# A second recorded order for a five-engine kernel of a long convolution and a SwiGLU block

## The chip, the cores and the metric

The kernel runs on one core of one Trainium2 chip. The metric is device microseconds (us) of one execution, the median of several; beside it stands one execution taken with the hardware profiler. Engines are PE (TensorE matmul), PEld (its weight loads), DVE (VectorE), ACT (ScalarE), POOL (GpSimd) and SP (SyncE, which here only issues DMAs).

## What is computed

```python
# S = 2048 tokens, D = 640, F = 1728, everything bf16
x  = A_q
h  = x + A(layernorm(x), k, v, shift_k, ssm_k, ssm_D)
h2 = h + (silu(layernorm(h) @ w_gate) * (layernorm(h) @ w_up)) @ w_down

def A(q, k, v, shift_k, ssm_k, ssm_D):
    k_shift = sum(k shifted down by i rows * shift_k[:, i] for i in 0..3)
    kv = k_shift * v
    y  = causal convolution of kv with ssm_k along S (length-2S FFT per channel)
    return q * (y + kv * ssm_D)
```

## The kernel before, in words

The 2048 tokens are four blocks j of 512; the 640 channels are two halves c of 320. A block's convolution is done with a 1024-point transform that is written as two small dense matmul stages, so it costs matmuls, PSUM evictions, elementwise products of spectra and SBUF-to-SBUF shuffles. All code is one function; every step is registered as an op with a name, and the names are used below:

- `kvm`, `kva`, `kvv` + jc (kv_block): the shift and the product kv, nine DVE operations of 128x1280 for each half.
- `s1X`, `s1K` + jc + b (fwd): first transform stage on PE, evicted by `e1..`; then `sh..G` DMAs that shuffle partitions; `s2X`, `s2K` + jc + G: the second stage, evicted by `e2..`. For block 0 the stages K01, X00 and X01 are done in one dense stage from the 1 MB table `full`, with no shuffle.
- `sw..` DMAs swap even and odd partitions; `m`, `a`, `q`, `x` operations on DVE multiply and add spectra (prods).
- `i2` + jc + G: first inverse stage on PE, evicted by `e3..` and shuffled by `rs..` DMAs; `i1` + jc + bp: second inverse stage. `q..`, `o..`, `h..`, `bn..`, `ag..` finish the first residual and the statistics of the second layer norm.
- `hn..` normalize; `tr..` (PE, block 0) or `hx..` (DMA, blocks 1 to 3) transpose; `gu` + j + i + bank: gate and up matmuls of feed-forward pair i, evicted by `si..`, `ue..`, multiplied in `gm..`; `dn` + j + b: down projection; `fa..` adds the residual, `st..` stores.

PSUM holds four two-bank tiles, two in pool pF and two in pool pC. SBUF pools have one to five slots, so many ops also wait for the last reader of the slot they take: KIN and VIN (loaded k and v) have one slot each, HT (input of `i1`) and the two TB tiles one each.

What sets the order is a table. `replay` (line 107) unpacks, from the string `_ORDER` (line 1133), the engine and a planned start for every op. Each engine's program is its ops sorted by planned start; there is no other scheduling, and every engine runs its list strictly in that order, waiting on semaphores. DMA issues stand in the same lists of SP, ACT or POOL, so a DMA that has to wait holds everything behind it on that queue. The planned starts do three more things:

```python
            o.lead = max(0, int(gap / (0.083 if o.start > cold else 0.166)))
...
            if held and max(held) > o.start - 1.0:
                continue
            k = bisect.bisect_left(work, (o.start - 0.2, 0)) - 1
            if k >= 0 and (not held or work[k][0] > max(held)):
                o.deps.setdefault(self.ops[work[k][1]], 2)
```

First, `lead` is a number of filler matmuls (128x192, line 521, results unused) that PE runs just ahead of an op, until the first `gu`, wherever the plan has PE idle. They are meant to keep its clock up, and they are part of PE's list: an op behind them starts after them even when its data is there. Second, a DMA that the plan issues late is given an artificial wait for an ACT or DVE op that ends about then. Third, the slot that a pool hands to a tile follows the planned order, so it decides which earlier reader is waited for.

Of the kernel before, what the change touches and what calls it, by code (L numbers as in the profile page):

```python
# [342 lines left out]
def bass_sequential_preLN__ssm_conv_h3__swiglu_ffn__prompt_kernel(  # L343
# [787 lines left out]

_INFO = None
_ORDER = (
    "c-pO#2UwHW8po6G3y_da_TGyuNJ0o?k_{w4AS93=OGHJ%0cxw#QneQMDr&1(rPhTLs#c#`N3FA3ZLO`>)oUw`)}mEvwT|Ly_1fOv-p6yE=e*~6&;K3g_ni-b"
    "!C)W&c`%_6C<uc>9#0q)27<kZFyNU1{=S3!F74I+5%%B!26@&2z#dpA<Z<BB`5@0l!k%+LpNj+mXz$sRetIRahpj&97=(e4#{=3c`=3nj`oQ!y`t0&B>0dMW"
    "qu1W?=ldtueCB4)c!9@PdBE)HGA|_glcY~4@1^%x^=S7(NIm)hz4dwp50`&L3HJ1hcm(C?*YTHvC(q!CeIX@*|0)3fhA8l&h(1CJ{+~pjZT(ODPku`16Wu@I"
    "2mEKEhuDDU3j=@hfu5lSJf;Qw?fO@oB+U7cYG?#f1&Kg7KqGJosslQpccCF*2@ruC@AX~)5MU257F2++7#wH={XlixQfMXG1ZxChp~s-R0WE42LLGMru{drU"
    "+!y;%EEzow`EL9~WB@Y*y&2tx=>n|ao8V>83TuH~hE0hX4DJTyF(YFtVy?tg!ZyUXVf$cdv4+^Su`}R{;tJs7<0$Y?;BLhCar@zm;F0(n@neyDka$!F5<umk"
    "W+8SUMj-AWir_!Rlj9c0Ns#ZM+~`&`9J3sA49&p|#2m%MVOy{jxHWhrkx$r!X~%8FH6#otU`gK+>@g!^yJEv}`{UT~2Dl1w9}L49W9nmLVo$}j#W$mL@tfj1"
    "5p&VSn1fg{?miB{<>SWSS0j|jX|aiMhfxtU7Rg3$LVbqagG(Yb5e^di6FwxoP8?2DCafjhBIS}Vl6R1sNU?-6GLABV(nAqZBa{lt2udTRjl!m;P*+h;QDrng"  # L1140
    "H9{RgJ50S!-A3!79i>U=_4Fgylaz4@?bI-9Cl^Y(#+}4D!vVQG-b~pp*-m+uVlI6c;}CrXqn!pa%IN8g>x|bK3)thBw;2xBQg#bV$a#~qhwm3G=U(D;3Z*=^"
    "=q)K;iV<%R(`3n#m9k0>lr0hN7p8M(iRfazs7+*$7-f9%4OwR*oZpYPLUuyX#XBlcB~~Y5mBUp9>JH5@bxBfl@=c9TOHxCU6`C~~P-~N?C=M$Js?5nFW9f)|"
    "@Fmn_Oag8^q7?fh>R0+bMizmEK8yYVvx=@~PhqhWj<d7aL)b&O?;y^@@$swT&BzwyWn>9T9bbdrh*x1>!7jsJ!{5Z%v8DtM@na%_7?1fBV?@tImt$sPI#J)E"
    "f><(kHr9-9CHz7-Pa=|$_$dA=j*EYfyahjs{5D}VrGly>en~w?Q_=y3lJ+*uz=V+V$P35^$dH7-33rHcQW-@?rqTtBjf@U@gt?xHW)-tGvk$Tq>>jp&2j>xa"
    "6#i9yg#aVe3uo{#qOF2a!f~SOqBkV#Bt+~)EER{vSK+_J%M-RGB$J%f8Ps~pN0gP6TNF6;Aax==p8h`bCuSTmmFOT|A(99#!fV70L@%938OhvD|B=aJRWs)@"
    "*Rig#&N6bDZ?KGP3Fin$%pJ+y&TZyh6&Qs_g>!^1kwV<gUnI~7Dg{%yr?^?X2|S9BBe*O4hPP65Q5+ImBugdTl8E%AL@u2#-5}eWs7{=kXppaz(-m7462ZO1"
    "eR6_gj^bOzJY|376a`YbT{%;^QAt(JR9RKsstz?y)uC!tgKDYzin=`MLeh?;G0A;WuIYwr?`lt{H0rkM_ot-jp@x>!z53S-)bv>G1YIcoUj|ajx%6GeRVIpg"
    "jfH02Xnxz;Cu4~oo!VrCo2I8Wn+{kS(}>0{+gH{WW43*<W4yWBTxuI+S!fAac^Q1iap%h}(DS`F=sxAX>z$Z+Dsy|rD|U)=gzM+5CXdCtB$J<|%T^|^X-Mj)"
    "v<&X6{Bb&38b5V}USxPRjcZnz@D@aRj8$$uX>BC#A*PZRkl3^aS_OSD!^UXff5QKqSHKT(7jto(Ce8`L0)bFcDe-VV<kYfT*^}5O*oQgyICF$u;^R`Lv_*Vg"
    "JX*X;%#uu#G)mV<7fWiyMA=souC!B%l$FcQ%LYno61x-2<@e>eiWKDug-}_W#8&QA9+fXu+Z9|DF)=SuC=bdzm7r>VuYZfetnjP0s^Zl>YD?0aNvD&<$zzhg"  # L1150
    "NS0~d(uB0^)FT?YcCt1@dp2dVc9@>28>U-lOSVNV2<t7|TN!x{se@$Cw=c2wSU1~Wa&)_HI_#`l%z3OUtN{BA+sa$c*NI|eBV=b)iE5+j8`Y1AGv(@}2DMXn"
    "F=dPTqWXMNYVtNknR1a@nAD*8C0VcO(DfvXG<Z#gW}xnb?wmGFzfUXHx9PX)z?7Dh9({AFHI;4{V%Te7rCmx}mM*k$(`(YZtgY!U87HQ#Gj*j`n{K6FHU3~^"
    "ni@>snP!+qn@5?38+M!Ln$<?B#b;}?HCfJ@(bn14i`GdQCo)9#{EXI&3mH2ywz?7acJCQ`tLKzstz(s=$Ki6m?EKQX#@XQ<<NU^v?7ZjHxWw-5E|DwZy5OpF"
    "&2drOH{5b}foF<4>Snv!-JR~Q-F}bNTj8nm9`TIJ>&{!1OU|1bIFolLaM<VZ^~*V$v&<jJ-I;sZAM&FLYVu2S^ub6N$X=Qq4crUN^G(g~Q!uYkURV+aL(~vh"
    "w7E!@)sm$v+7~8g1I43@w+Fil#)U=}ejl_Hg5kNv%OVS-!jhAH78kK2>gf9Du3AJ1txsZUdnvSRR!Li*d8O2{x-vTln_REFFZVg4Mx`%3a6flV?zFtc0cPRs"
    "pr*It<ihoZ!jOzl6*LP<h3^aB5r3ierCimy(`KbDH5^K-HJmo=O1BtomNZk3?N{UL*7LT}sh3k{TMk(qwtAa3qpy9f^Nu6dp?4g#@iIzX(_IssVpo&nYgf?I"
    "<EiwTGjDj0WDd^SnT7L3eO<n~>@C>}AKaVj6?p5tHJR5k_j-T!uFp1Qg?#bZt9{-6IDejhnSVh}L#{b6J7CTY<SocM6h0Kr4=yjH6!kB<UX)*K4SyDD4%Ua}"
    "hA)O^6j_Uorb_jnr3KS}G5O7P_Dc6FmUo<&oflkV-7NP9ZjXJqV|X^)BlPdfIp@`6R(U!+6EinvVzMk*A7s_|R`@pN8vQl?U49^^(|6sMne$zaFDETGKgXT7"
    "FmFZRZtjgdL;ivMmkT~FKozblxLt5KxHoV!a4zs#{_%W5!L@u|!SVb-1)(51xH>qy@MK|6Fex-KBnpoR?+SN^(!vwMjADJUthm1T<KmmeibybWyLfe^tT-uh"
    "ECP?3qE*qckx7xIk=DqrNK(`pZHc}c<(AxzLQ7aBq!MGvqLPl1^CkZ-DeW`9ic-btKczpcA8Nquis=<M`&SJZQ~BM1P38QG_P*A>Z58q=PjzSYih;x$ZU2^<"  # L1160
    "%yL-SkpZTG2g*MjSY7#fWnI6M{R;X<t525=E9<T*E&r)3wR~v5rW(>9M(x5{NL}k7(cra%)wL69adp#&kcZA6dSz&H?fg34khUQ=hx`VQutdZ"
)


# [26 lines left out]
```

## Time and profile before

| what | value |
|---|---|
| median of 5 runs | 305.59 us (303.33 to 310.04) |
| the profiled execution's own time | 304.88 us |
| its span, first to last instruction | 303.0 us |
| PE busy | 279.7 us (92%), 1696 matmuls, 74 of them fillers |
| DVE busy | 235.7 us (78%), 413 instructions |
| ACT busy | 184.4 us (61%) |
| POOL busy | 22.6 us (7%) |
| DMA | 52.08 MB in 55292 packets |

PE's busy time counts the modelled, overlapping length of matmuls. The distance from one matmul's start to the next is the better measure, and the trace gives it for all 1696. At full clock it is 136 ns for 320 columns, 216 ns for 512 and 83 ns for a filler; in parts of the first 75 us it is twice that (267 ns and 160 ns).

### The profile page before, as it was taken

How to read it: one execution, taken by the hardware profiler on the slowest of the kernel's cores; microseconds unless marked ns; L12 is line 12 of the kernel's file. 1: busy time of each engine (PE TensorE's matmuls, PEld its weight loads, DVE VectorE, ACT ScalarE, POOL GpSimd, SP SyncE). 2: the span in 40 equal slices, each digit the busy share in tenths (PEclk: the TensorE clock that was granted, in tenths of full speed). 3: DMA queues.
4: the chain of work that ended last, by engine and by line, in shares of the span. 5: the costliest groups of instructions: out<-in, count | busy, mean ns of one | idle time of the engine just before them, and what ended most of it. 6: DMA issues, size and time to landing. Idle time of an engine off the chain costs nothing.

```text
span 303.0 us, 4816 instructions
## 1 busy us (share of the span) xinstructions
PE 279.7 (92%) x1696; PEld 162.0 (53%) x1696; DVE 235.7 (78%) x413; ACT 184.4 (61%) x273; POOL 22.6 (7%) x29
## 2 busy tenths in 40 slices
PE   7799977387999999998999999999999999999993
PEld 4655544145555555664454567754554675444671
DVE  2798989769979998999989999969799963033322
ACT  3556676548799878763899878857887521511000
POOL 0000022012040000120000200100002010000000
PEclk9999999879999999999999999999999999999998
DMA  7967699958889957998724344558221132000011
GB/s 226 312 186 254 225 271 253 298 209 240 300 262 343 278 208 219 285 178 274 240 108 130 110 153 135 148 190 267 110 108 45 44 78 75 0 0 2 0 66 43
DMA packets 55292, 52.08 MB, mean 172 GB/s; under 512 B 19923, under 2 KB 49140, under 8 KB 55269
## 3 DMA queue, kind: packets, MB, share of 16 engines
q1 hardware_dynamic: 53444, 46.47, 49.0%
q0 software_dynamic: 960, 3.41, 4.6%
q10 hardware_dynamic: 864, 1.90, 1.9%
q8 instruction: 13, 0.21, 0.3%
q14 instruction: 11, 0.08, 0.1%
HBM read 19.00 MB, written 2.62 MB: 71 GB/s over the span
## 4 chain that ended last, share of the span: by engine, by line
PE 64%; DVE 15%; DMA 10%; ACT 4%; issue 4%; SPq 1%; ACTq 0%
PE ps L498 62%; DVE sb L507 12%; DMA sb<-sb 6%; ACT sb L481 4%; DMA sb<-in_A_k_dram 2%; DVE stt L761 2%; DMA tab<-cst_tab 1%; SPq L489 1%; PE ps L521 1%; PE ps L630 1%; DVE stt L765 1%; ACT sb L484 0%; DVE sb L783 0%; DVE stt L776 0%; ACTq L489 0%
## 5 line engine op out<-in xcount | busy, mean ns | idle before, releaser
L498 PE MATMUL ps<-sb 128*128 128x320 bf16 (+3 forms) x1128 | 209.9, 337 | 3.8 <-DMA sb<-in_A_k_dram 1.2
L507 DVE TENSOR_TENSOR sb<-sb 128x1280 bf16<-128x1280 bf16 (+2 forms) x238 | 174.0, 768 | 13.7 <-ACT sb L1056 3.4
L498 PEld LDWEIGHTS ps<-sb 128*128 128x128 bf16 (+3 forms) x1128 | 108.8, 98 | 86.4 <-issue 4.3
L481 ACT ACTIVATE sb<-ps 128x640 bf16<-128x640 f32 (+1 forms) x134 | 90.5, 714 | 37.9 <-PE ps L498 35.6
L498 PE MATMUL ps<-sb,tab 128*128 128x320 bf16 x450 | 79.4, 305 | 10.6 <-ACT sb L481 3.7
L498 PEld LDWEIGHTS ps<-sb,tab 128*128 128x128 f16 x450 | 41.7, 99 | 42.3 <-issue 7.2
L507 DVE TENSOR_TENSOR sb<-ps,sb 128x640 bf16<-128x640 f32 (+3 forms) x34 | 29.1, 860 | 41.1 <-PE ps L498 39.0
L1040 ACT ACTIVATE sb<-ps 128x1024 bf16<-128x1024 f32 (+2 forms) x32 | 29.3, 917 | 27.3 <-PE ps L498 27.2
L484 ACT ACTIVATE sb<-ps 128x640 bf16<-128x640 f32 x29 | 19.5, 703 | 10.8 <-PE ps L498 10.7
L1056 ACT ACTIVATE sb<-ps 128x1024 bf16<-128x1024 f32 x18 | 18.4, 1022 | 9.1 <-PE ps L498 7.1
L761 DVE BATCH_NORM_STATS2 stt<-sb 128x6 f32<-128x320 bf16 x48 | 22.4, 483 | 0.1
L784 ACT ACTIVATE sb<-sb,stt 128x320 bf16<-128x320 bf16 (+1 forms) x26 | 19.1, 754 | 4.2 <-DVE stt L776 3.4
L774 POOL TENSOR_TENSOR stt<-stt 128x2 f32<-128x2 f32 (+1 forms) x10 | 10.7, 1071 | 67.4 <-DVE stt L772 52.7
L521 PE MATMUL ps<-sb 128*128 128x192 bf16 x74 | 10.5, 299 | 2.9 <-ACT sb L481 1.4
L521 PEld LDWEIGHTS ps<-sb 128*128 128x128 bf16 x74 | 7.8, 118 | 5.4 <-ACT sb L481 2.4
L482 DVE CAST sb<-ps 128x640 bf16<-128x640 f32 x6 | 4.8, 821 | 4.3 <-PE ps L498 4.2
L783 DVE TENSOR_SCALAR sb<-sb,stt 128x320 bf16<-128x320 bf16 (+1 forms) x22 | 7.9, 380 | 0.1
L810 POOL TENSOR_TENSOR stt<-stt 128x4 f32<-128x4 f32 x2 | 3.1, 1530 | 59.7 <-DVE stt L808 59.7
L803 ACT ACTIVATE sb<-sb,stt 128x640 bf16<-128x640 bf16 x8 | 6.6, 827 | 0.0
L796 ACT ACTIVATE sb<-sb 128x640 bf16<-128x640 bf16 x8 | 5.9, 734 | 0.0
L765 DVE BATCH_NORM_AGGREGATE stt<-stt 128x2 f32<-128x12 f32 x24 | 4.3, 196 | 0.0
L489 POOL DMA_DIRECT2D tab<-cst_tab x2 | 1.3, 634 | 35.8 <-ACT sb L481 25.2
(29 smaller groups left out, 30.8 us busy)
## 6 DMA issues: line engine op xcount, KB each, us to landing
sb<-sb SPq DMA_DIRECT2D x144, 160.0 KB, 2.5
sb<-in_A_k_dram SPq DMA_DIRECT2D x5, 560.0 KB, 5.0
out_dram<-sb SPq DMA_DIRECT2D x16, 160.0 KB, 2.1
sb<-in_A_q_dram SPq DMA_DIRECT2D x3, 640.0 KB, 5.0
sb<-sb SPq DMA_DIRECT2D x24, 80.0 KB, 3.0
sb<-in_B_w_up_dram SPq DMA_DIRECT2D x3, 480.0 KB, 5.2
sb<-in_B_w_down_dram SPq DMA_DIRECT2D x3, 480.0 KB, 5.3
sb<-in_A_v_dram SPq DMA_DIRECT2D x4, 320.0 KB, 4.3
```

The costliest lines, as they stand in the source:

```text
L481: fns = {"act": lambda a: a.activation(out=dst(), in_=src(), func=ACTF.Copy), "dve": lambda v: v.tensor_copy(out=dst(), in_=src())}
L484: fns = {"act": lambda a: a.activation(out=dst(), in_=src(), func=ACTF.Copy, scale=scale), "dve": lambda v: v.tensor_scalar(out=dst(), in0 ...
L498: return lambda t: t.matmul(o(), l(), r(), start=st, stop=sp)
L507: return lambda v: v.tensor_tensor(out=o(), in0=a(), in1=b_(), op=op)
L521: P.fill = lambda t, pt: t.matmul(B32(pt, 1, 192), V(GUT, 13 * 512 + 256, 128), V(GUT, 13 * 512, 192), start=True, stop=True)
L761: vec(dve1(CW, False), lambda v: v.bn_stats(st6(l, j, b, c), V(xt, b * D + c * CW, CW)), [(xt, (b, c))], [(ST, ("s", j % 2, b, c))], prio, ...
L765: vec(0.16, lambda v: v.bn_aggr(ag(l, j, b), st6b(l, j, b)), [(ST, ("s", j % 2, b, c)) for c in range(2)], [(ST, ("a", j, b))], prio, name ...
L774: P.op({"pool": 0.95}, lambda g: g.tensor_tensor(out=y, in0=va, in1=stt[:, 288:288 + hi - lo], op=ALU.pow), c1 + [(ST, "half")], c3, prio, ...
L783: "dve": lambda v: v.tensor_scalar(out=dst(), in0=src(), scalar1=tmv(l, j, 5)[:, b:b + 1], scalar2=rs(l, j, b), op0=ALU.add, op1=ALU.mult),
L784: "act": lambda a: a.activation(out=dst(), in_=src(), func=ACTF.Identity, scale=rs(l, j, b), bias=tmv(l, j, 3)[:, b:b + 1])},
L1040: P.op({"act": act_c(n)}, lambda a: a.activation(out=dst(), in_=src(), func=ACTF.Silu), rd, wr, -1000, name=f"si{j}{i}")
L1056: P.op({"act": act_c(1024)}, lambda a: a.activation(out=V(ut, 0, 1024), in_=B32x2(u, 512), func=ACTF.Copy), [(u, 0), (u, 1)], [(ut, 0)], - ...
```

## The change

Only the string `_ORDER` differs. The functions, the set of ops, their shapes and their data dependences are the same. The diff, cut:

```diff
 _ORDER = (
-    "c-pO#2UwHW8po6G3y_da_TGyuNJ0o?k_{w4AS93=OGHJ%0cxw#QneQMDr&1(rPhTLs#c#`N3FA3ZLO`>)oUw`)}mEvwT|Ly_1fOv-p6yE=e*~6&;K3g_ni-b"
...
+    "c-pO#2UwHm7J$hhWG93qBxI1ifJ_oX0!awjB#=NzNJ2tnh%!__Y_Iavs@3bNlWOa#qu5^cs;ISfkGikp7OjKY)=|;cs<^M#;sr-9wt8!yr{Dkl=bY#J&N<&X"
...
 )
```

Unpacked, the new table does this:

- **Engines.** 18 ops go from DVE to ACT (the evictions tap0, tap1, e300G2, e330G2, e331G0, e2X31G1, e2X31G2, e2K31G3 and ten norms `q`). 13 go from ACT to DVE (the evictions e2X10G0, e1X20b0, e1K30b2, e330G0, e330G3, e331G1, e2K31G1, e2K31G2, e2X31G3, three norms `q`, and hn23).
- **DMA queues.** tab1, tab3 and wdl go from POOL to SP; tab2, shK00G0, shK00G2 and rs00G1 from ACT to SP; shK00G1, rs00G0, rs01G0 and rs01G1 from SP to ACT; x1, kin21, x2, kin31 and vin31 from SP to POOL.
- **First part, SP.** ident and drow stand ahead of kin0 and kraw00; vin10 and kin10 are issued right behind `full`, ahead of the first shuffles; the transposing load kx10, which followed x0, is now behind shK00G2 and shK00G0. vin10 has an artificial wait for he01, and x0 for the first kvm00.
- **Fillers.** 76 for 74, elsewhere: 23 (for 14) before the tap matmuls, none (for 5) before hl01, 2 before ktr00, 21 (for 4) before ktr01, none (for 3 + 3 + 9) up to s1X10, 2 (for 8) before i1001, 4 before i201G3 (14 before s1X11b2 gone), 5 (for 10) before i1010, 14 (for none) before s2K10G1, none (for 4) before s1K11, 3 + 2 around tr00.
- **Local swaps.** PE's order changes by neighbours in most places: i200G1 comes one dense stage earlier, i201G1 before i1000, s1X11b0, s1X11b2 and s2X10G3 before s2K10G0. Up to the first `gu` PE has the ops that it had there before, and i210G0 besides; the order of the feed-forward pairs is nearly the same.

More of the change, by code (lines that the diff above doesn't have):

```diff
@@ L1133 @@
 _ORDER = (
-    "c-pO#2UwHW8po6G3y_da_TGyuNJ0o?k_{w4AS93=OGHJ%0cxw#QneQMDr&1(rPhTLs#c#`N3FA3ZLO`>)oUw`)}mEvwT|Ly_1fOv-p6yE=e*~6&;K3g_ni-b"
-    "!C)W&c`%_6C<uc>9#0q)27<kZFyNU1{=S3!F74I+5%%B!26@&2z#dpA<Z<BB`5@0l!k%+LpNj+mXz$sRetIRahpj&97=(e4#{=3c`=3nj`oQ!y`t0&B>0dMW"
-    "qu1W?=ldtueCB4)c!9@PdBE)HGA|_glcY~4@1^%x^=S7(NIm)hz4dwp50`&L3HJ1hcm(C?*YTHvC(q!CeIX@*|0)3fhA8l&h(1CJ{+~pjZT(ODPku`16Wu@I"
-    "2mEKEhuDDU3j=@hfu5lSJf;Qw?fO@oB+U7cYG?#f1&Kg7KqGJosslQpccCF*2@ruC@AX~)5MU257F2++7#wH={XlixQfMXG1ZxChp~s-R0WE42LLGMru{drU"
@@ L1138 @@
[L1138 to L1161, printed above, removed]
+    "c-pO#2UwHm7J$hhWG93qBxI1ifJ_oX0!awjB#=NzNJ2tnh%!__Y_Iavs@3bNlWOa#qu5^cs;ISfkGikp7OjKY)=|;cs<^M#;sr-9wt8!yr{Dkl=bY#J&N<&X"
@@ new lines @@
+    "?|*(E7z_phV*pPd5E$^>1V3NE7Z&JOE9QT$fPP_p2Yvd54RD_mFs3i8_ppDynBPSLejf?=Z6pZTn+@>1p1xv1Pih7Asopo{*#h*sy_V{geF_Nvjd+q240;s<"
+    "aDQ6Av!4|9yiIU_CNJy)pSAM5rPoUic)jF(IG@1-^rQF8>#6mZkODmc4+8Wq;1lsGO2C&k)qf(MLg_ypuXK1>d#}mv)mH-l^p*XI_Fn$i5bYa0(ElR}{NvH+"
+    "%?y0ma6D}Z`0MNe|HSM8UzX_EX9d2v|KzWKJzBs&l&|8nf^t8m1`v$tdnN$KfldRVplv`4Xe;OvxH9GwKxND<&~DIT&?Qg=%#1w}>w`EzTc9I=WvIvC(*PoH"
+    "Iq(?Rgld4nVHcovP%G>*d_NL|*2A(;W6)jb_t0C=^_Y_&4tNy!ORz9@bnK~EF@yqc0xyNc$6bl_#8p9#LqL$(kZ<A^$9))gA2td0IqW8MBuoy!2Hy)C3WvZA"
@@ new lines @@
+    "h|`FjNE|APnuI)oWTNb_HSku%9t0l&K;DXz!Li7VC<MA4O~KS)8qwdPMVLd_HtZQJC%zmvH(@+J5etYP8}CS1jo(3-OV|r}6GDw^j5{31g3f_nflZ1%AA14P"
+    "85e~<g04XrkW}P6)L8gE^g=W?J{V8OEx^u=|33ahxE4_pr-9u^veA{OOQ<8LAeM-uCVZ1nM(9j<4}TFK#^)2iBB~P?kxr0$Nc9PA2~$XX@;LHV@_R{5<Wb~*"
+    "l0PMPl5>;%NqCBl(n{Hxlu0S3xF}7ORH}hGow}QfrhSLqPF|gGIH@$5$0if+u#P2j7!TQM&fwGx;ik0vX%DFxbSEu_UO=5in?OBC8%xL2Madu0vB{|nA9H51"
+    "owbx5=Em@v*&VF6dH2|R_@h!VDQ5*^g^yCQMGdKV)&@ok{|ryWrU@d#D}1luy6}V43Sm;(`LuU9Bn~re0~gLs<t<6ulU6AGKz2dis*ETA=^K>+)ge`rd~!NY"
@@ new lines @@
+    "iBe5fjTMI__oP3{bm@{<0hj`vj%vkV;=OP)<|J+)^)3yGZ^i`BwS-1`4gD7?E4iK7!{9LYGUvg}@P+Vc2qtnQ@)oil)dO$Cb>q4)`PfT1X#x-XF197%YXXz7"
+    "kWhn}hmoU~qOYM(VJ@R8&=puNb_w=!{35~;!qLQ@#BK4Dao@+6;2fk2I5&w&$V)nqbQ&L~Y@#fqc2mjJO6of54~bc%JW>m(FoA}T63|2=c^`>EKTjD+kENZY"
+    "S0~>~wli88JCfmy4u*|$j(wi(=a9J5xFFtq!EDaYoMpUgJSRU_G(x;lgu?E??8Y|5ABumB+nu1o+ll*0@#K5tl}WS7KPHuuKPHc$s410ndh%?%hY%)yLA;2^"
+    "5opBmL@_NVaVh;AeF&YAJc)ju{yyUXLq;1zo0?2y4rlFT`PeY_FYF3V9Z$?(&o}ei`1OKITs7|?_W@VWp2!Ze4|5*y^gNefBX6Hzkq|4qBMgb!L=7o3MVCa1"
@@ new lines @@
+    "lsbN@@ZGf2X^X`K$y5nIdXYa;z?1w<B9ji3mdmb6Mbe=3qV%j3AnTM>$g%PRa<k%sEL}cRK1set-lABaeoc|6Y)QYUenb68H7KJd^GXIyTadXWbGx=so2AiZ"
+    "Ey$jsLa4DiQPvdo44q#;D#v4(W+dd&jB|3An_D#k4PC!WZ`T?PUl~=|>vXG33v(yyJr;?TW;|_xnI0Lh=9r8JO_wc0ZFalQamdMbtaKc47Px@!@n(Ug%Sy0M"
+    "br$5Ioei#AE_Z$)VOr94GLp8E)x+$_SdevFb3r>_)0#awN32iD`6T<O@wPG1^b<itoI$)w>>{tHx@jwDb+m4dmdoe9!Ck<*&iaChVtv5{@Ky@03LY?pEG@H^"
+    "$zZNvj$y53ZQ+gJH1ktZcM7@%)xuwdHsNmJ9T7JrPjr*NCgq%{R-{gOCxwyPp4yQDO%sR@i7CA-H%Ko@+N5`-c-d5$PI5}|xg<*tNjok^NHmhSWXEL{vRN{P"
@@ new lines @@
+    "Y>g~MK12GxT&$R)V5AR8-;|C~)++ZX*{XU~cV<AfN)@Bd&KRLyt_ozH%t%u!O?9TrIirm*bBkGKnP$0QCR<E7+l*C~jh0$#tMzemdvcJ`&Ok8BnMatpT%oWc"
+    "b#*F4zFD3vzb|)+=ZbeLV$z`*mW(b1RB2Q+DmtZb8AP#0fmL-V^Hu9IM=Rr0^OT2_H!`lPPh_NIsxsfn5NmFzFqzq!4oz75KzlpWo7J7=$X=EW*3}r#WasKq"
+    "jSafFdbX~`fY3_}%k@9%r|7%%O2ZPvHp5Q_t-+zq%-L_)u8ZdIOruTXj4N|+xkGag=H{E1nZ*{8xx&28yu&&nugkp9dCu~{F0|gV46|;wqHSi|N48NmtL-h@"
+    "TI<i&i?%xZzwK@IuWiR{Rd%#pVP9llXK!{89A_N)4vXU-jwO!$4rkt%dC@$Kb5>rbcZj#E2vxMUc$Ig8Z=5^Py`)fC81XQR<`f}3vpi>g#lG={;*z&RRr$IC"
@@ new lines @@
+    "OYzZSx%-4~mA^XhbBQKY61);P9CDU+<UerXN|%QU3+9*33UBnYN{$D<Dp^`03gm>Yg=@=hmo-O8<)ceSM0z4!WxnzO(dzOW<-;mIYWgACFyP^UQRN-wJDJ#Y"
+    "rC2X*w64(Hafgb*-hdZYyw?W}%<?Pz%>j5&65J77&Dq4Q<Hhis`C!4Mj9qG-`f)GkIa#-}Vzf)LT68ycpBO(gY|?*d8k74VSEX&!J~T>lXP9=Hy3J_wTedn2"
+    "%Cg?lY<g_EZ{yp&woh#UYm@yK$A9wN&IPW^PGkQ3d{e=>f?@7`?iB@h3v%42^2(j-oDi4KHQseQkL8?}f5OFc-_76bUh0YScs<uW;|l*)w5KSscx{o<JKx(G"
+    "+7{YdGBG%{ba(0CupxXr*d3f!Vh@r-_d{1p@!^S@k26<lJF^pV?&ZkM?T%eKoW06^&7R@dXg}m=x0G9<E_lI&g1;Bdaqe@b=T+o=>q6&iTzg%%f;|Ob&l&F<"
@@ L1162 @@
+    "p6#9<kGk-NJJ~}nv=>e<L=@dEI#xK{d$kx<yrekOcf>c^f5UGJ*!|iPc%aZ*QoODh?bG-M`*!&f{iVJk{&N2{|Adn7N@@aI1H|C4AUNa?Eejn9l0sD>NvWjt"
+    "?eM?Cw1_t{G14CKMc$2k7KTN@W!kctWn0U>j$DpN${s~nWs}Nolr1V7740cgM72?Wv>@6XJrmUpxE`H9fIeXRpp?NkYC^Ru2cNA~4qQ4AS--fBRXw#nTy?Oj"
+    "tGaNIW8m>Yin{%^TZg!ZY^ci~I==E|<@fb();CmD4H;RDt{zvDSo5$NR7<X0RWWz)2bF1+jg^Tt!l65cT8AANHn3^Ku)Phg#-ojbrnOD#;X8*Lo8NEFYS`Rp"
+    "Y}(UA9sXbA<6`L"
 )
```

## The prediction

> **What bounds the kernel now.** I read the page first, then PE's busy time by stretches of the run, then the chain that ended last, then the timeline where the chain names a wait, and last the start of every single matmul.
>
> ```profile
> span 303.0 us, 4816 instructions
> PE 279.7 (92%) x1696; PEld 162.0 (53%) x1696; DVE 235.7 (78%) x413; ACT 184.4 (61%) x273; POOL 22.6 (7%) x29
> ```
>
> ```profile
> PE   7799977387999999998999999999999999999993
> DVE  2798989769979998999989999969799963033322
> PEclk9999999879999999999999999999999999999998
> DMA  7967699958889957998724344558221132000011
> ```
>
> PE has holes only in its first ten slices; DVE is nearly full from slice 3 to slice 30. By stretches (columns: stretch, length, PE busy and count, granted clock, DMA share, GB/s):
>
> ```profile
> 0.00:15.00 15.00, 11.56 (x68) 1.00 0.90 271
> 15.00:30.00 15.00, 14.38 (x93) 1.00 0.72 215
> 30.00:45.00 15.00, 12.06 (x87) 1.00 0.79 248
> 45.00:60.00 15.00, 8.63 (x61) 0.94 0.98 274
> 60.00:75.00 15.00, 11.83 (x84) 0.83 0.70 223
> 75.00:303.00 228.00, 221.23 (x1313) 0.99 0.47 147
> ```
>
> Matmul starts say it more sharply. Counting columns / 2.4 GHz as useful, fillers as lost, PE loses 11.3, 3.4, 5.0, 9.9 and 7.8 us in the first five stretches, 37 us in all, and only some 4 us from 75 us to its last matmul at 297.9. So two things set the time: when feed-forward work starts (the first `gu` is at 72.9), and whether PE then stays fed by a DVE that is nearly as full. The chain, in the first 75 us (start, length, what):
>
> ```profile
> 1.60 6.97 DMA sb<-in_A_k_dram
> ...
> 37.50 4.11 DMA tab<-cst_tab
> ...
> 50.10 6.14 DMA sb<-sb
> ```
>
> and the timeline behind the third of these:
>
> ```profile
> 56.29 0.72 PE L498 MATMUL ps<-sb,tab 128*128 128x320 bf16 x4 [3.13 <-DMA sb<-sb]
> ...
> 60.13 1.80 PE L521 MATMUL ps<-sb 128*128 128x192 bf16 x10
> ...
> 61.73 2.34 PE L498 MATMUL ps<-sb,tab 128*128 128x320 bf16 x8
> 63.03 0.82 DVE L507 TENSOR_TENSOR sb<-ps,sb 128x640 bf16<-128x640 f32 x1 [3.28 <-PE ps L498]
> ```
>
> The 6.14 us DMA is shK10G0: issued at 50.10, it shares the engines with kin20, issued by POOL at 49.83, and lands at L = 56.24. Then come s2K10G0, three first-stage transforms that wait for PSUM slots, ten fillers at 160 ns, i1010 at half clock, and a DVE that stood idle 3.28 us for it. o011, the last link before block 0's statistics, starts at 65.84, L + 9.6.
>
> **What the Trainium skill says.** *TensorE: Matmul & The Clock Gate*, Part 1: PE runs at half rate until it has been busy for about 3.4 us, and drops back after an idle window of that length. The trace agrees: spacing of 320 columns goes from 267 to 137 ns at 13.85, 5.2 us after steady work began at 8.62, and back to 267 at 59.86, after 3.4 us and 1.4 us of idle. *DMA: Bandwidth & Descriptors*, Queues, rings and completion order: each DMA engine takes packets of its queues in turn. The trace agrees: from 52.5 to 55 the 1280-byte packets of shK10G0 and the 4480-byte ones of kin20 run at about 35 each per half us. *VectorE: DVE Perf Modes*, Why PSUM operands drop a tier: a PSUM source slows DVE; here a 128x640 eviction takes 821 ns on DVE, 702 on ACT.
>
> **The change, part by part.** The sum is against the profiled execution: 304.88 us, span 303.0. It is 0.7 under the median, so sums may read 0.7 low.
>
> *DVE's load.* After kin0 lands, 6 evictions (start to start 0.74) and 10 norms (0.28) leave, 4.4 + 2.8 = 7.2; 9 evictions, 3 norms and one 0.36 arrive, 7.9. Net +0.7 us. The taps' two evictions also leave, but ended at 6.98, before kin0 (8.57): worth nothing. Up to hn01, DVE has 2.1 - 1.5 = 0.6 us less.
>
> *Start.* ident stands before kin0 on SP: one issue of 0.47, so kin0 lands about 9.05 (8.7 if packets rather than issue bind). hl01, hl02 and a tap are six matmuls at 267 ns: 10.65. Two fillers 0.3, ktr00 12 x 107 ns: 12.25; hl11: 12.5. Now 21 fillers. With the clock turning 5.2 us after 9.05, 11 run at 160 and 10 at 83: 2.6 us, to 15.1 (all at 160: 15.9). kraw01 landed at 11.06 before and at about 12 now, so the fillers, not data, hold ktr01: 15.1 for 12.11. Then ktr01 0.7, kte01 1.24, he12 0.7 and the first e1K00 0.6 on ACT: s2K01G0 at 18.3 for 16.30, **+2.0** (+2.9 at the cold end).
>
> *Dense stretch.* From s2K01G0 to i200 took 16.9 us; one dense stage of 1.1 us now comes after it, and 3 fillers of 0.25 us are gone: 18.3 + 15.5 = 33.8 for 33.2, **+0.6**. kin10 and vin10 land by about 20 instead of 23.5 and 30.1, but DVE waited only 0.39 us for kin10 and not for vin10: nothing.
>
> *tab3.* On SP behind rs00G1 it lands near 38.5 for 41.62. The 1.75 us that PE waited for it go, and so do 9 fillers (0.75 us). Late next is ACT: five evictions of 0.6 stand between s2X01G3 and the slot that s1K10 takes, and rs00G2 still lands behind kin11 and swB011 near 42.6. That puts i1000 at 43.8 for 43.34: **+0.5**.
>
> *e2X10G0 on DVE* stands behind o000, kvm11, kva11, mi0110, h000: 44.5 + 0.8 + 3 x 0.74 + 0.4 + 0.8 = 48.7 for 47.94 on ACT. Behind it wait s1K10b2 (its PSUM slot) and swX100, and shK10G0 behind swX100 in SP's queue: issued 50.4 for 50.10. kin20 on POOL waits for the fourth kvm11, behind e2X10G0: 50.6 for 49.83. So the shuffle, issued 0.3 behind kin20, is now 0.2 ahead. The trace has no such case. Lower bound: its packets pass alone in about 0.6 us, L = 53.3. Upper: interleaved to the end of kin20, L = 57.2. A POOL issue takes 1.7 us to its first packet and a shuffle 2.4, so they still overlap: L = 56.2, **no change**.
>
> *From L to gu000.* s1X11b0, b2 and s2X10G3 now run before L; s1X11b3 and b1 and 5 fillers follow s2K10G0: i1010 at L + 2.7 for L + 5.5. Of that, 14 fillers before s2K10G1 (1.2 to 2.2 us) and s2K10G3 ahead of i1011 take back most: o011 at L + 8.9 for L + 9.6, **-0.7**. h011 now stands before va10: **+0.4**. The extra kva20 before nm10 hides under POOL's power (1.02 us in its row). gu000 near 72.6, -0.3.
>
> *After gu000.* Work on PE is the same. I compared, for each PE op that needs a DVE result, its margin before with the change in work ahead of it on both engines. dn010 and i220G2 had 0.06 us margin and get 0.5 to 0.6 us more DVE work ahead: about 0.5 lost near 131 to 138. Near 232, i231G3 had 0.1 and gets 1.4 more, but DVE idles 2.5 and 1.8 us at 204 and 214 and can use some: 0 to 1 lost. I take **+0.6** together, -0.3 to +1.5 as ends; the lower because the few us PE loses there could shrink. kin21, x2, kin31 and vin31 on POOL stand before powers that are due later: nothing, unless such a wait is late, when the power and its norm are late with it.
>
> Sum: -0.3 + 0.6 = +0.3, 305.2 against 304.88 and 305.9 against the median; I say 305.5.
>
> **Rivals.** *The fillers cost in full (slower).* In place of the last chain's absorption, ktr01's 3 to 3.8 us pass on: clock cold throughout s2K01G0 at 19.2, i200 at 34.7, then every `rs` and `kin` a microsecond later, e2X10G0 at 50, L near 58.5 rather than 56.2, and o011 with it. That is 2.3 more at gu000, and with DVE at its 1.5: 305.2 + 2.3 + 0.9 = 308.4, or 309 with fourteen cold fillers. It decides when L passes 58.5. For it: PE was without a gap over 1 us from 16.3 to 34. Against: tab3's removed wait. *The shuffle slips ahead of kin20 (faster).* L = 53.3, PE's idle before it is too short to lose the clock, i1010 and the following run at 136 ns: -2.9 - 0.7, gu000 near 69, if wu0 and shK10G1 are there; 301.5 to 302. Against: 2.4 us to a shuffle's first packet. *DVE is the bound after 75 us*: all its extra work shows, and POOL's new loads hold a power: +2, 307. *The orders are equal in effect*, since most moves are between neighbours: 304.9.
>
> **How the numbers follow.** Forecast and equal orders 0.40, DVE-bound 0.12, full fillers 0.26, slip 0.22. One per cent, about what a measurement of this kernel can tell from no change, is 302.5 to 308.6. Most of the slow rival lies past it, as does most of the fast one; some of DVE-bound does too: faster 0.22, same 0.52, slower 0.26. The likeliest case alone is 304 to 307. The range takes in both rivals but their outer tails: 301.5 to 309.5.
>
> **What would show it.** Right: ktr01 near 15 behind 21 fillers, s2K01G0 near 18.3; no wait for tab3; shK10G0 landing near 56; o011 within 9.2 us of that; gu000 within 1.5 us of 72.6; PE losing 4 to 5.5 us after it. Wrong: L under 54.5 or over 58, a clock that stays full through 56 to 66, or gaps of over 1 us in PE's list after 80 us.

## The result, and the profile after

| | before | after |
|---|---|---|
| median | 304.70 us (79 runs, 302.12 to 310.41) | 306.86 us (44 runs, 304.47 to 309.99) |
| ratio after / before | | 1.0074, 95% interval 1.0059 to 1.0089 |
| profiled execution, its span | 304.88, 303.0 us | 308.29, 306.5 us |
| mean PE clock, median of the runs | 0.985 (runs taken with the experiments) | 0.978 |

The kernel became slower by 0.74%, 2.2 us. Ratios, here and below, leave out the runs that are more than 1.5% above the fastest of their kernel; medians take in all. The two profiled executions differ by 3.4 us, because that of after is 1.4 above its median; what follows is worked out between these two and then tested on medians.

The page of after, span, busy times and the rows of the 40 slices:

```profile
span 306.5 us, 4836 instructions
PE 282.6 (92%) x1698; PEld 163.5 (53%) x1698; DVE 235.2 (77%) x408; ACT 186.3 (61%) x278; POOL 25.5 (8%) x31
...
PE   7998867677989999998999999999999999999993
...
DVE  0797789959699999998999999987799963033421
...
PEclk9999997788999999999999999999999999999999
DMA  7967589868979975669861415656421122000011
```

Busy times are those of before within 3 us, and from slice 11 on PE is as full as it was. The first ten slices differ: PE's holes lie elsewhere in them, and the clock is down in four (7 to 10) rather than two (8 and 9). By stretches, in the columns used before:

```profile
0.00:15.00 15.00, 12.32 (x88) 1.00 0.86 289
15.00:30.00 15.00, 13.49 (x83) 1.00 0.67 195
30.00:45.00 15.00, 11.82 (x78) 1.00 0.71 223
45.00:60.00 15.00, 10.08 (x51) 0.79 0.96 280
60.00:75.00 15.00, 11.42 (x73) 0.84 0.73 213
75.00:306.00 231.00, 223.45 (x1334) 0.99 0.48 148
```

From 45 to 60 us PE is busier than before (10.08 for 8.63) with fewer matmuls (51 for 61): it works at 0.79 of the clock. Busy is not the same as done. The third view is the chain of waits, whose rows before named three DMAs; these belong to its places in after (start, length, what, count; pieces named issue left out):

```profile
11.65 0.27 PE ps L498 x2
11.92 2.14 PE ps L521 x21
14.06 0.68 PE ps L630 x12
...
44.34 0.70 PE ps L498 x4
...
49.85 2.04 PE ps L498 x8
...
52.51 1.02 ACT sb L784 x2
53.60 0.69 ACT sb L484
...
55.42 0.60 ACT sb L484
56.07 0.46 PE ps L498 x2
56.55 0.71 ACT sb L481
57.40 1.30 PE ps L498 x4
58.73 0.71 ACT sb L481
59.49 1.31 PE ps L498 x4
60.80 0.80 PE ps L521 x5
61.60 1.07 PE ps L498 x4
62.66 1.79 PE ps L521 x14
64.45 0.28 PE ps L498 x2
```

No `tab` transfer is left in it, and no shK10G0 either: from 50 to 60 us the chain goes to and fro between PE and evictions (lines 481, 484) and norms (line 784) on ACT. Line 521 is the filler: results nobody uses are a link of the chain, for 2.14 us before ktr01 and for 1.79 us before s2K10G1, the two longest after the start. The starts of single ops set the prediction's figures beside the traces (us; a DMA by its landing; "carried" is after less before):

| op | predicted | before | after | carried |
|---|---|---|---|---|
| kin0 lands | 9.05 | 8.57 | 8.00 | -0.6 |
| ktr01 starts | 15.1 | 12.11 | 13.90 | +1.8 |
| s2K01G0 starts | 18.3 | 16.30 | 17.41 | +1.1 |
| i200 starts | 33.8 | 33.19 | 34.08 | +0.9 |
| i1000 starts | 43.8 | 43.34 | 45.22 | +1.9 |
| e2X10G0 ends | 48.7 | 47.94 | 50.53 | +2.6 |
| shK10G0 lands (L) | 56.2 | 56.24 | 57.60 | +1.4 |
| s2K10G0 starts | L | L + 0.0 | L + 0.4 | +1.7 |
| i1010 starts | L + 2.7 | L + 5.5 | L + 3.8 | -0.3 |
| o011 starts | L + 8.9 | L + 9.6 | L + 10.0 | +1.7 |
| gu000 starts | 72.6 | 72.91 | 75.70 | +2.8 |
| last down projection ends | 0.3 later | 297.85 | 301.16 | +3.3 |

In this pair of executions, then, most of the loss is there before the first `gu`: 2.8 of 3.3 us. The timeline of PE and DVE in after from 57 to 66 us (start, length, engine, line, idle time before and who ended it) shows the second of the two filler groups:

```profile
57.40 1.29 PE L498 MATMUL ps<-sb,tab 128*128 128x320 bf16 x4 [0.89 <-ACT sb L481]
...
59.49 1.31 PE L498 MATMUL ps<-sb,tab 128*128 128x320 bf16 x4 [0.80 <-ACT sb L481]
...
60.59 1.01 PE L521 MATMUL ps<-sb 128*128 128x192 bf16 x5
...
61.39 1.27 PE L498 MATMUL ps<-sb,tab 128*128 128x320 bf16 x4
...
62.46 1.99 PE L521 MATMUL ps<-sb 128*128 128x192 bf16 x14
62.70 0.82 DVE L507 TENSOR_TENSOR sb<-ps,sb 128x640 bf16<-128x640 f32 x1 [1.43 <-PE ps L498]
...
64.29 0.71 PE L498 MATMUL ps<-sb,tab 128*128 128x320 bf16 x4
...
65.50 0.83 DVE L507 TENSOR_TENSOR sb<-sb 128x1280 bf16<-128x1280 bf16 x1 [1.97 <-ACT sb L481]
```

i1010 is the four matmuls at 61.39, s2K10G1 and G2 the four at 64.29. shK10G1 had landed at 60.88 and the PSUM slot was free at 61.16, so nothing but the fourteen fillers kept s2K10G1 from 62.5 or so: 1.6 to 1.8 us. The bill is on DVE: the product mr1000 at 65.50 waits for the eviction of s2K10G1, and DVE stands idle 1.97 us, after 1.43 before the o010 at 62.70.

### The profile page after: what moved, and what is told of

It reads as the page before. It is cut to its first block, busy times and chain, and to the rows that moved or that the text cites. A ratio compares the mean times of both kernels' runs of the same rounds, so it can differ in the third digit from the quotient of the medians.

```text
span 306.5 us, 4836 instructions
## 1 busy us (share of the span) xinstructions
PE 282.6 (92%) x1698; PEld 163.5 (53%) x1698; DVE 235.2 (77%) x408; ACT 186.3 (61%) x278; POOL 25.5 (8%) x31
## 4 chain that ended last, share of the span: by engine, by line
PE 81%; ACT 9%; DVE 3%; DMA 3%; issue 2%; ACTq 0%; SPq 0%; DVEq 0%
PE ps L498 77%; ACT sb L481 5%; DMA sb<-sb 3%; PE ps L521 3%; DVE sb L507 2%; ACT sb L484 2%; ACT sb L784 2%; PE ps L630 1%; ACT L1040 0%; ACTq L489 0%; ACT sb L1040 0%; ACT sb L1056 0%; DVE stt L761 0%; PE ps L994 0%; DVE stt L765 0%
## 5 line engine op out<-in xcount | busy, mean ns | idle before, releaser
L498 PEld LDWEIGHTS ps<-sb 128*128 128x128 bf16 (+2 forms) x1128 | 109.6, 98 | 83.9 <-issue 2.6
L481 ACT ACTIVATE sb<-ps 128x640 bf16<-128x640 f32 (+2 forms) x133 | 89.7, 715 | 44.5 <-PE ps L498 35.0
L498 PE MATMUL ps<-sb,tab 128*128 128x320 bf16 x450 | 82.2, 310 | 14.2 <-ACT sb L481 7.6
L784 ACT ACTIVATE sb<-sb,stt 128x320 bf16<-128x320 bf16 (+1 forms) x32 | 22.2, 727 | 2.2 <-DVE stt L776 2.2
L521 PE MATMUL ps<-sb 128*128 128x192 bf16 x76 | 11.5, 318 | 2.4 <-DVE sb L520 1.2
L521 PEld LDWEIGHTS ps<-sb 128*128 128x128 bf16 x76 | 9.3, 130 | 4.4 <-ACT sb L481 1.5
L783 DVE TENSOR_SCALAR sb<-sb,stt 128x320 bf16<-128x320 bf16 (+1 forms) x16 | 6.1, 394 | 0.3
L489 POOL DMA_DIRECT2D sb<-in_A_q_dram x3 | 1.9, 619 | 49.6 <-DVE sb L507 49.6
L489 POOL DMA_DIRECT2D sb<-in_A_k_dram x3 | 2.9, 967 | 28.1 <-DVE sb L507 25.2
```

The costliest lines, as they stand in the source:

```text
L481: fns = {"act": lambda a: a.activation(out=dst(), in_=src(), func=ACTF.Copy), "dve": lambda v: v.tensor_copy(out=dst(), in_=src())}
L498: return lambda t: t.matmul(o(), l(), r(), start=st, stop=sp)
L521: P.fill = lambda t, pt: t.matmul(B32(pt, 1, 192), V(GUT, 13 * 512 + 256, 128), V(GUT, 13 * 512, 192), start=True, stop=True)
L783: "dve": lambda v: v.tensor_scalar(out=dst(), in0=src(), scalar1=tmv(l, j, 5)[:, b:b + 1], scalar2=rs(l, j, b), op0=ALU.add, op1=ALU.mult),
L784: "act": lambda a: a.activation(out=dst(), in_=src(), func=ACTF.Identity, scale=rs(l, j, b), bias=tmv(l, j, 3)[:, b:b + 1])},
```

## The experiments

The theory: the time is lost in the head (all that precedes block 0's tr00, the transpose ahead of the first `gu`), and there by fillers that stand in PE's list before ops whose data is there. The rivals: the changed order after 75 us (more DVE work ahead of PE's needs); the eviction e2X10G0 moved to DVE, which holds shK10G0's issue; the lower clock by itself, whatever the order.

**Which half of the order.** Two grafts. Both tables are unpacked, and the planned start of tr00 cuts them: ops ahead of it take engine and start from one table, the rest from the other, shifted.

```diff
...
-        for o, e, s in zip(self.ops, eng, start):
-            o.eng, o.start = self.ENG[e], 0.01 * int(s)
...
+        for o in self.ops:
+            i = o.idx
+            if i in rank:
+                o.eng, o.start = self.ENG[e1[i]], max(s1[i] + t0 - t1, t0) + 1e-6 * rank[i]
+            else:
+                o.eng, o.start = self.ENG[e0[i]], s0[i]
```

Old head, new rest:

> The old order up to the planned start of tr00 (block 0's first transposes), the new order from there on. Theory H (the loss arises ahead of the first feed-forward matmul): about the kernel before, 304.5 to 305.3 us. Theory R (the new order of the rest, with more DVE work, loses it): 306 to 307.

Measured: 304.30 us, ratio to before 0.9987 (0.9958 to 1.0017), span 303.2.

New head, old rest:

> The new order up to the planned start of tr00, the old order from there on. Theory H: 306.2 to 307, the first gu near 75.5 us. Theory R: about 305.

Measured: 307.76 us (6 runs), ratio 1.0115 (1.0059 to 1.0171), span 305.1. With the old head the new rest costs nothing that can be measured; with the new head the whole loss is there. The head it is, and the rival "after 75 us" is out. What that rival rests on does occur: PE waits 1.12 us for DVE at 84.8 in after, and as long at 81.4 in the graft with the new rest, without a price in the time. And a loss of the head need not show in full at the first `gu`: in the trace of the new head with the old rest gu000 starts 1.1 us later than in that of before, and the last `dn` ends 2.1 later.

**Which fillers.** In the kernel after, single filler counts are set by name once the leads are computed:

```diff
+        for o in self.order["pe"]:
+            o.lead = LEADS.get(o.name, o.lead) if o.lead or o.name in FORCED else o.lead
```

First `LEADS = {"s2K10G1": 0}`, the fourteen:

> The changed kernel without the 14 fillers ahead of s2K10G1. If the fillers hold the path (s2K10G1's shuffle had landed at 60.87 and its PSUM slot was free at 61.14, fillers ran to 64.27): s2K10G1 right behind i1010, near 62.7, everything behind it 1.6 us earlier, 305.3. If DVE or the statistics of block 0 are late for another reason: 306.9, no change. A third way: a colder clock behind it eats the gain.

Measured: 305.20 us, ratio 1.0023 (0.9998 to 1.0047). Its timeline, PE and then DVE:

```profile
60.21 2.34 PE L500 MATMUL ps<-sb,tab 128*128 128x320 bf16 x8
62.90 1.22 PE L500 MATMUL ps<-sb,tab 128*128 128x320 bf16 x6 [0.35 <-ACT sb L483]
```

```profile
61.52 0.82 DVE L509 TENSOR_TENSOR sb<-ps,sb 128x640 bf16<-128x640 f32 x1 [0.84 <-PE ps L500]
62.79 1.23 DVE L509 TENSOR_TENSOR sb<-sb 128x1280 bf16<-128x1280 bf16 x2 [0.45 <-ACT sb L483]
```

i1010, s2K10G1 and s2K10G2 are now one run of eight from 60.21, and DVE's wait for the product's input falls from 1.97 to 0.45 us. o011 starts at L + 7.9 rather than L + 10.0.

Then `LEADS = {"ktr01": 4}`, four fillers for 21, as before the change:

> The changed kernel with 4 fillers ahead of ktr01, as before, for 21. If the late start of the dense stretch (17.39 for 16.30) is carried through to the end: about 1 us less, 305.9. If a DMA (swB000 landing at 32.21, kin11 at 42.98) takes over as the wait: 306.9, with s2K01G0 near 16.3 and the loss gone by i201.

Measured: 306.11 us, ratio 1.0053 (1.0027 to 1.0079). In its timeline ktr01 is the twelve at 12.35, for 13.90 in after:

```profile
11.71 0.85 PE L523 MATMUL ps<-sb 128*128 128x192 bf16 x4
12.35 1.44 PE L632 MATMUL ps<-sb 128*128 128x128 bf16 x12
```

The 1.5 us at ktr01 are 1.3 at i200, 1.2 at i1000, 2.2 at L and 1.9 at gu000 in the profiled execution; the medians show 0.75 of it. The interval overlaps with that of after, so the share of this group by itself is not settled.

Both edits together:

> The changed kernel with both filler edits: none ahead of s2K10G1, 4 ahead of ktr01. If the two costs lie one behind the other on one path, they add: 305.2 - 0.8 = 304.4, at or a little under the kernel before. If the rest then waits for DVE, whose lists are full, 305.2 stays.

Measured: 304.41 us, ratio 1.0006 (0.9974 to 1.0037): equal to the kernel before. By ratios to before, the fourteen take 0.51% away, the seventeen 0.21%, both 0.68%, of 0.74%; what is left is within the interval. The median clock of this kernel's runs is 0.978, the very value of after, and its time is 2.4 us lower: a lower mean clock by itself was not what made after slow.

Its trace holds one thing more. shK10G0 and kin20 were issued at the same moment, 50.08, and the shuffle landed at 53.67, ahead of kin20 (55.54), which is the prediction's "slip". s2K10G0, which needs the shuffle, started at 56.50 all the same, with s2X10G3 in these four:

```profile
55.91 1.29 PE L500 MATMUL ps<-sb,tab 128*128 128x320 bf16 x4 [0.89 <-ACT sb L483]
```

It was waiting for its PSUM slot, which an eviction on ACT freed at 56.36.

**The other direction, fillers into the old order.** Before, with `LEADS = {"s2K10G1": 14}`:

> The kernel before with 14 fillers added ahead of s2K10G1. If the price of those fillers is theirs alone, and not a matter of the new order: +1.6 to 2.2 us, 306.6 to 307.2. If the old order has slack there: 305.

Measured: median 307.04 us for 304.67, 2.4 up; in the profiled execution gu000 is 1.7 us later. Its ratio, 0.9951 (0.9908 to 0.9994), says the opposite, but rests on 5 of the 22 runs: four took 301.45 to 302.84 us at a clock of 0.991 to 0.997, the fifth 305.69, and the 17 left out 306.0 to 310.3. So the direction in most runs is that of the theory, the size is not to be had from this kernel, and the test counts as inconclusive.

**Taking out the old order's own cold fillers.** Before, without the ten of i1010 that the prediction showed at 60.13:

> The kernel before without the 10 fillers ahead of i1010, which stood behind them from 60.1 to 61.73 with its data landed at 58.94. If fillers on the path cost what they take: 1.6 us less, 303.3. If DVE or a shuffle is next (shK10G1 at 58.54, e1X11b1 at 60.09 are there): still 303.5. If they keep the clock up: no gain, or a loss.

Measured: 304.73 us, ratio 0.9990 (0.9960 to 1.0020), a miss. gu000 starts 2.1 us earlier, as it should, but the chain does not keep it. On DVE the lead is 1.8 us from 66 to 88, 1.5 at 105, 1.8 at 128 and 1.1 at 140. On PE gu120 starts at 139.14 for 140.17, 1.0 us earlier, behind waits of 0.57 and 1.15 us, where the kernel before has one of 0.79 (for a shuffle):

```profile
124.51 0.98 PE L500 MATMUL ps<-sb 128*128 128x320 bf16 x6 [0.57 <-DMA sb<-in_B_w_down_dram]
```

```profile
139.14 1.67 PE L500 MATMUL ps<-sb 128*128 128x512 bf16 x7 [1.15 <-ACT sb L486]
```

The first is for a load of w_down, the second for an eviction on ACT. DVE was busy 61.49 of the 65 us from 75 to 140 in the kernel before, and 60.94 here, with little room to run ahead. And the clock of its runs is 0.979 for 0.985. Between the profiles of before and after a delay of the head passed through this stretch whole (2.8 us at gu000, 3.3 at the end); of the gain, 2.1 us, the profiled execution has 1.0 left at its end, and the median nothing.

**e2X10G0 back on ACT**, in the kernel after:

```diff
...
+        o, p = by["e2X10G0"], by["e2X10G1"]
+        o.eng, o.start = "act", p.start - 0.001
...
```

> The changed kernel with the one eviction e2X10G0 back on ACT, right ahead of e2X10G1; nothing else moved. If its place behind o000, kvm11, kva11, mi0110 and h000 on DVE made shK10G0 and s1K10b2 late: about 0.7 us less, 306.2, shK10G0 issued near 51.5. If ACT, with two shuffle issues ahead of it there, is as late as DVE: 306.9.

Measured: 306.82 us, ratio 1.0059 (1.0035 to 1.0082). The eviction ends at 49.29 for 50.53, shK10G0 is issued at 51.98 for 52.64 and lands at 56.54 for 57.60; gu000 gains 1.0. But i1000, which runs ahead of the eviction, was 0.5 us earlier too (44.71 for 45.22), so only 0.7 us at the eviction's end and 0.5 at the landing can be the move's. In the times this is 0.15% with overlapping intervals: a share of the loss at most, not settled.

**How far does it go?** After with four fillers at ktr01 and none behind it (30 are gone there):

> The changed kernel with 4 fillers ahead of ktr01 and none behind it (its 26 later ones are gone). If fillers cost only what they hold up, and the 14 and the 21 were what held the path: as with those two edits alone, 304.4. If the other 12 keep PE's clock up through the waits near 50 to 70 us: slower than that, 305 to 306, with more half-clock windows.

Measured: 304.65 us, ratio 1.0023 (1.0003 to 1.0044), no better than the two groups alone. Before without its 51 fillers behind ktr01:

> The kernel before without its 51 fillers behind ktr01. If they keep the clock up: more half-clock windows between 30 and 70 us and 305.5 to 307. If they only fill waits: 304.7, or 303.5 since the 10 ahead of i1010 held the path.

Measured: 303.85 us, ratio 0.9963 (0.9938 to 0.9988). Most of the old order's fillers buy nothing, then; the clock of its runs fell to 0.9785 and it still gained.

**Fillers where PE waits anyway.** Before, 34 fillers put ahead of s2K10G0, into the wait for shK10G0:

> The kernel before with 34 fillers (2.8 us) added ahead of s2K10G0, in the 3.4 us in which PE waits there for the shuffle shK10G0. If the clock lost near 58 us is what costs most in the head: it stays up in most runs, i1010 and its followers run at 136 ns, 302 to 303. If the window that decides lies behind that wait: no change, 304.7. If the shuffle often lands sooner than in the profile: slower, up to 306.

Measured: 304.28 us, ratio 0.9960 (0.9929 to 0.9992), median clock 0.992: a small gain by the ratio, 0.3 us by the medians. The profiled execution took 306.00 us; in it the clock was down from 58.6 to 65.4 all the same, and i1010 ran at half rate. The same, and without the ten cold fillers of i1010:

```diff
+LEADS = {"s2K10G0": 34, "i1010": 0}
+FORCED = ("s2K10G0",)
```

> The same, and the 10 fillers ahead of i1010 gone. If the head is the bound: 1 to 1.5 us under the version with them, near 301.5. If DVE, whose lists are full from 75 us on, is the bound (taking the 10 away alone brought the first gu 2.1 us forward and the end not at all): no more than that version.

Measured: 302.22 us, ratio 0.9931 (0.9896 to 0.9967), faster than both kernels. Its clock row, and its PE from 52 to 62 us:

```profile
PEclk9999999989999999999999999999999999999999
```

```profile
52.61 2.97 PE L523 MATMUL ps<-sb 128*128 128x192 bf16 x34
57.34 0.72 PE L500 MATMUL ps<-sb,tab 128*128 128x320 bf16 x4 [1.76 <-DMA sb<-sb]
...
60.51 2.83 PE L500 MATMUL ps<-sb,tab 128*128 128x320 bf16 x10 [0.89 <-ACT sb L483]
```

The 34 end 1.7 us before the shuffle lands, so they hold nothing; the clock is down in one slice rather than two, and the runs' median clock is 0.995. In the profiled execution gu000 is 1.05 us earlier and the last `dn` 0.7 us, less than the 2.4 us between the medians. b_no10 has its order without the 34 fillers, 304.73 us at a clock of 0.979: here, between two kernels that differ in fillers off the path, the clock is a likely cause of the 2.5 us between the medians (0.6% by the ratios, whose intervals just touch), but no run held it fixed.

## Why the prediction was wrong, step by step

*Start.* Fillers, not data, hold ktr01: right. The size was off by 1.2 us, since kin0 landed at 8.00 (ident ahead of it on SP cost nothing to be seen) and the clock rose at 12.6. s2K01G0 moved +1.1, not +2.0.

*Dense stretch.* +0.6 predicted, +0.9 measured, but by another way: one us less came in and 0.2 rather than 1.4 us of it were absorbed. What the step took off as removed work came back as waits that it did not have: DVE stood idle 1.60 us for swB000, which landed at 32.23 (28.02 before) beside the x1 transfer that POOL had issued ahead of it, at 25.76, and 1.52 us for an ACT eviction.

*tab3.* The wait is gone from the chain, as predicted; i1000 is not at +0.5 but at +1.9. a_ktr4 has it at +0.6, so a part goes with the first group. The three other kernels that have the new order and the 21 fillers up to here have it at +0.8 (new head, old rest), +0.9 (a_no14) and +1.4 (a_e2act): single executions of one order differ by 1 us here, and the profiled one of after is the latest.

*e2X10G0 on DVE.* +0.8 predicted, +2.6 measured, of which 1.9 came in with i1000; a_e2act puts the move itself at 0.7 us. The rest of this step was wrong in the favourable direction: the order of kin20 and shK10G0 did not turn over (issued at 52.23 and 52.64), and L took up half of the 2.6. That left L 1.4 us late, where the step had "no change".

*From L to gu000*, the step that failed. It counts from L, as if the landing of shK10G0 were still what s2K10G0 waits for. In the old order it is: in the seven traces with the old head s2K10G0 starts 0.04 or 0.05 us after L. The new order puts s1X11b0, s1X11b2 and s2X10G3 ahead of it, and s2K10G0 takes the PSUM slot of s1X11b0. In the seven traces with the new head it starts 0.14 or 0.15 us after the eviction that frees this slot, 0.4 to 2.8 us after L; in after the slot came free at 57.85, 0.25 us after the landing. The work moved ahead of L, booked as 2.8 us gained at i1010, had become the wait. The gain was 1.7: i1010 came at L + 3.8 and not at L + 2.7. Of this 1.1 us, 0.4 is the wait for the slot; another 0.5 goes with the clock, which in after fell at 57.0 already, ahead of s2K10G0 (a_no14, where it fell at 59.5, has i1010 at L + 3.3).

The fourteen fillers, in turn, were priced rightly: from i1010 to o011 the prediction has 6.2 us and the trace 6.2, and a_no14, without them, 4.6. What failed was the gain that was to pay for them, so o011 stood at L + 10.0 for L + 8.9 and the term **-0.7** is +0.4. h011 before va10, +0.4: +0.4 measured between o011 and hn01. From hn01 to gu000 the prediction put nothing; it is 3.60 us for 2.95. PE now has i210G0 and i210G1 between tr00 and gu000, where it had i210G1 alone: gu000 starts 0.4 us after the eviction of tr00 before, 0.6 in the four kernels of the new order whose clock was full there, and 1.1 and 1.2 in after and a_ktr4, which have a second cold stretch (74.1 to 77.5 us in after). So -0.3 at gu000 became +2.8: 1.4 at L, 1.1 at i1010, 0.7 behind hn01.

*The clock.* *TensorE: Matmul & The Clock Gate*, Part 1, of the Trainium skill ties the clock to windows of about 3.4 us, and the traces agree to the digit that can be read: every half-clock stretch between the start and the end of a run, in all fourteen traces here, lasts 3.4, 6.8 or 10.2 us. So here a clock once lost was gone for 3.4 us at least. The prediction read the trace of before as agreeing with a drop after an idle window too; there the trace is less clear, for the clock fell at 58.3 though PE had been busy for 1.3 of the 3.4 us before that. How thin the feed has to be for the clock to fall is not shown.

*After gu000.* +0.6 predicted, +0.5 in the profiled execution (3.3 - 2.8), by luck: 0.5 us of work (i210G0) had gone ahead of gu000, and against it stand the half clock up to 77.5 and the wait of 1.12 us for DVE at 84.8, longer than the gap of 1 us that the prediction gave as a sign of being wrong. The old head with the new rest gives 0.9987 (0.9958 to 1.0017), so no cost can be shown at all; half a microsecond would be inside the interval. (The "some 4 us" that PE loses from 75 us on is 7.4 if it is counted as in the five stretches ahead of it; nothing hangs on it.)

The sum was +0.3 where the chip gave +2.2 by the medians and +3.4 between the two profiled executions. *The rivals.* "Fillers cost in full" had the right direction, and its rule was wrong: L never reached its 58.5, it stayed at 57.60, because two thirds of the loss came at the fourteen fillers behind L, not through ktr01 ahead of it. The rival was built on the larger group, and the smaller group, which stood on the chain's last link, cost more: 0.51% for fourteen, 0.21% for seventeen. The slip of the shuffle did not happen in after. In a_no14_ktr4 it did, and brought gu000 to 72.19, not near the rival's 69, since the slot and not the shuffle held s2K10G0. The DVE-bound rival was out by the graft. What remains unsettled: how much of the e2X10G0 move is in the 0.74%, what the norms moved to ACT (1.02 us of the chain at 52.5) cost, and the 0.06% that both filler groups leave.

## What to carry to other kernels

Work put on an in-order engine to keep it warm is priced like any other op: ask of each group whether the op behind it has its data when the group begins, and where the next link of the chain is. Fillers inside a wait for a transfer hold nothing while they end before it lands, and are the only ones here that may have paid; on the chain they held the next op for their full length (1.8 us for fourteen, 1.5 for seventeen), and the cold ones take 160 ns rather than 83. When a change moves work into a wait, ask again what ends that wait: here it was no longer the transfer but the slot that the moved work held, and times counted from the landing were wrong. A gain in the head has to get past every later wait, here a weight load, an eviction and a DVE that is 95% busy, before it is a gain at the end.

## What was not expected of the hardware

The time of one and the same program goes with its clock. Over 179 runs of the kernel before, taken beside the experiments, time and mean granted clock have a correlation of -0.67, about 2.8 us per 0.01 of clock: the nine runs at 0.991 and above took 300.9 to 304.8 us, those at 0.979 and below 303.3 to 310.7. Which of the two leads is not shown by that, and between kernels it is no rule: a_nolate at 0.971 took 304.65 us, and after at 0.978 took 306.86.
